# Rebuilding the last, short chunk of a speech joint kernel: one grad_out load, gradient row layouts by TensorE, x rows in another tile, and a transfer-grouping rule limited to the middle

## The chip, the cores and the metric

The kernel runs on one core of a Trainium2 chip. Its time is device microseconds (us) of one execution. Engines are named as in the profile: PE is TensorE (PEld its weight loads), DVE is VectorE, ACT is ScalarE, POOL is GpSimd, SP is SyncE, which here only issues transfers ("SPq" is its queue).

## The reference

The forward part is a small speech encoder with a joint network; the kernel computes the forward output and the gradients of all seven inputs (8 outputs in bf16).

```python
h  = gelu(conv1d(x,  w1))[:, ::2, :]     # x: (2, 16000, 256), 3 taps
f  = gelu(conv1d(h,  w2))[:, ::2, :]     # (2, 4000, 256)
j  = tanh((f @ w_f)[:, :, None, :] + (g @ w_g)[:, None, :, :])   # (2, 4000, 8, 256)
out = j @ w_o                            # out_0, (2, 4000, 8, 256)
# out_1 .. out_7: gradients for x, w1, w2, g, w_f, w_g, w_o, given grad_out
```

## The kernel before

**Chunks.** The 2 x 4000 output positions are laid end to end (8000 columns) and cut into 17 chunks: one of 256 columns, fifteen of 512, and a last one of 64 (lines 254 to 284). A 512-wide chunk is A = 4 blocks of Pw = 128 columns; the last chunk, number 16, is A = 1 block of Pw = 64, with one extra column (`c.ext`) for the end of x. Chunk 8 holds the border between the two batch entries.

**Stages of a chunk.** `stage_a` computes both convolutions with GELU and its derivative, the product with w_f (FE), and row layouts of the activations (HRo, HRe, FR). `stage_j` walks over four pairs of the 8 values of u. For each pair it computes tanh (tile JT, and JR in row layout on ACT), the output (OUT_SB), the grad_out product through w_o (matmuls of GOT with WOT, line 653), the derivative on DVE (NGZ, line 674), the sum over u (ZS, line 689, whose last addition writes NGFE, line 687), and the w_o gradient, which stays in one PSUM tile, GWO, for the whole kernel. `stage_de` goes backwards: GF from NGFE (line 753), GHe and GHo from GF (lines 770 and 801), the x gradient GX (line 867), and the weight gradients: ACCF (from NFR and FR), three ACC2 (from GFR and HRe/HRo), three ACC1 (from GHeR, GHoR and the x rows X, line 896). In the last chunk each of the seven weight gradients is finished by one DVE instruction into a stage tile (line 720) and stored.

**Row layouts.** A matmul contracts over partitions, so the weight gradients need NGFE, GF, GHe and GHo with columns on partitions. `rows` (line 457) makes these (NFR, GFR, GHeR, GHoR) with one transposing transfer each on SP's queue, for all 128 partitions whatever the chunk's width. grad_out comes in by `load_go` (one transfer per pair of u: tile GO) and is turned by `load_got` (one transposing transfer per pair: tile GOT); the class "go" has 3 buffers, "got" 4. `load_x` brings x rows into class "x" (2 buffers); class "xc" (1 buffer) holds the transposed x columns that `stage_a` reads.

**Order of the work.** All instructions are collected as `Op`s and then placed by a planner, `Flow.issue` (line 105). It keeps estimated times of every engine and of the transfer ring, and places, again and again, the ready operation that can start first; among equals the lower priority number goes first. That number is a position in the stream of columns (`F.now` or `at`): chunk k's work lies around its first column, the start at numbers below 256, the last chunk around 7936 to 8300. The order that it finds is the order on each engine's queue; real waits follow from the data. For SP it has a grouping rule (lines 150 and 151): plain copies are kind "D", transposing transfers kind "T"; while the current group has less than 6000 ns (D) or 7500 ns (T) of estimated work, an operation of the other kind counts as 2500 ns later than it could be.

In iteration k of the main loop (line 1010) the planner receives the loads of chunk k, `stage_j(k)`, `stage_a(k+1)` and `stage_de(k-1)`. So the end of the kernel is `stage_j(16)` beside `stage_de(15)`, then `gg_out` (gradients of g and w_g) and `stage_de(16)`.

Of the kernel before, what the change touches and what calls it, by code (L numbers as in the profile page):

```python
# [36 lines left out]
class Flow:  # L37
# [12 lines left out]

    def __init__(self, ctx, tc):
        self.ctx, self.tc, self.ops, self.slots, self.now, self.seq = ctx, tc, [], {}, 0.0, {}

    def cls(self, name, n, any_order=False, psum=False):
        pools = [self.ctx.enter_context(self.tc.tile_pool(
# [49 lines left out]
    def issue(self):  # L105
# [20 lines left out]
        while left:  # L126
            best = None
            for e, lst in avail.items():
                t, wake, cand = T[e], self.WAKE[e], None
                for o in lst:  # L130
                    s = o.ready + wake
                    for b in o.new:
                        st = seq[b.cls]
                        if not st[2] and st[1] != b.seq:
                            s = None
                            break
                        free = [x[1] for x in slots[b.cls] if x[1] is not None]
                        if not free or (st[2] and len(free) <= self.SPARE and queue[b.cls][head[b.cls]] is not o):
                            s = None
                            break  # L140
                        s = max(s, min(free) + wake)
                    if s is None:
                        continue
                    if o.work:
                        q = "SW" if e == "POOL" else "HW"
                        s = max(s, lanes[q][nlane[q] % self.LANES])
                    s = max(s, t)
                    k = (s, o.prio, o, e, s)

                    if e == "SP" and kind is not None and o.kind != kind and group < self.GROUP[kind]:  # L150
                        k = (s + self.WAIT,) + k[1:]
                    if cand is None or k < cand:
                        cand = k
                if cand is not None and (best is None or cand[0] < best[0]):
                    best = cand
            assert best is not None, "no operation can start"
            _, _, o, e, s = best
            for x in o.eng:
                avail[x].remove(o)
            for b in o.new:  # L160
                free = [i for i, x in enumerate(slots[b.cls]) if x[1] is not None]
                i = min(free, key=lambda i: (slots[b.cls][i][1], i))
                b.slot, slots[b.cls][i][1] = i, None
                seq[b.cls][1] += 1
                b.t = slots[b.cls][i][0].tile(b.shape, b.dtype, name=b.name, tag=b.cls)
            T[e] = s + o.cost[o.eng.index(e)]
            if o.work:

                if e == "SP":
                    group = o.work + (group if o.kind == kind else 0.0)  # L170
                    if o.kind == "T" and kind == "D":
                        ring += self.SKEW
                    kind = o.kind
                if o.kind == "T":
                    ring = max(ring, s + 300.0) + o.work
                    T[e] = max(T[e], ring - 1500.0)
                    o.done = ring + 1600.0 + self.SLACK
                else:
                    ring = max(ring, T[e] + 500.0) + o.work
                    if e == "SP":  # L180
                        T[e] = max(T[e], ring - self.HOLD)
                    o.done = ring + (2200.0 if e == "POOL" else 1300.0) + self.SLACK
                q = "SW" if e == "POOL" else "HW"
                lanes[q][nlane[q] % self.LANES] = o.done
                nlane[q] += 1
            else:
                o.done = T[e] + self.TAIL[e]
            o.span = (s, T[e], e)
            for c, q in queue.items():
                while head[c] < len(q) and q[head[c]].span is not None:  # L190
                    head[c] += 1
            o.fn(e)
            left -= 1
            for b in o.bufs:
                b.users -= 1
                if b.users == 0 and b.cls is not None:
                    slots[b.cls][b.slot][1] = o.done
            for d in o.succ:
                d.left -= 1
                if d.left == 0:  # L200
                    put(d)
# [16 lines left out]
def kernel(  # L218
# [28 lines left out]
    KT = 2  # L247
# [158 lines left out]
    def load_go(k, up, at, after=()):  # L406
        c = chunks[k]
        A, Pw = c.A, c.Pw
        GO = buf("go", [P, NB, 2, V], BF16, "GO")
        dma("SP", lambda: GO[:Pw, 0:A].rearrange("p a u v -> p a (u v)"),  # L410
            lambda: bass.AP(tensor=go_.tensor, offset=go_.offset + (c.c0 * U + 2 * up) * V,
                            ap=[[A * U * V, Pw], [U * V, A], [1, 2 * V]]),
            r=[], w=[GO], bytes_=Pw * A * 1024, new=[GO], at=at, after=after)
        st[k].setdefault("GO", {})[up] = GO

    def load_got(k, up, at):
        c = chunks[k]
        A, Pw = c.A, c.Pw
        GO = st[k]["GO"][up]
        GOT = buf("got", [P, NB, 2, KT, P], BF16, "GOT")  # L420
        dma("SP", lambda: GOT[:, 0:A, :, :, :Pw].rearrange("p a u k c -> p (a u k) c"),
            lambda: GO[:Pw, 0:A].rearrange("p a u v -> p (a u v)"), r=[GO], w=[GOT],
            bytes_=Pw * A * 1024, new=[GOT], transpose=True, at=at)
        st[k].setdefault("GOT", {})[up] = GOT

    def load_x(k, at, after=()):
# [3 lines left out]
        for h in range((A + 1) // 2):  # L430
            nb = min(2, A - 2 * h)
            nr = 4 * nb + 1
            X = buf("x", [P, 9, D], BF16, "X")
            row = 4 * c.c0 - 3 + 8 * h
            lo, new = 0, [X]
            if c.first and h == 0:
# [5 lines left out]
                    lambda row=row, nr=nr: row_ap(x_, row + 4 * A, 4 * A, 15, nr), r=[], w=[(X, "c")],  # L442
                    bytes_=15 * nr * 512, at=at, after=after)
                lo = 16
            if c.last and h == 0:
                p0 = c.Pw // 32 * 32
                zero(lambda X=X, p0=p0: X[p0:c.Pw + 1], [(X, "m")], new=new, at=at)
                new = []
                dma("SP", lambda X=X: X[c.Pw:c.Pw + 1, 0:3], lambda: x[B - 1:B, T - 3:T, :], r=[(X, "m")], w=[(X, "b")],
                    bytes_=1536, at=at, after=after)  # L450
            dma("SP", lambda X=X, lo=lo, nr=nr: X[lo:c.Pw, 0:nr].rearrange("p f d -> p (f d)"),
                lambda row=row, lo=lo, nr=nr: row_ap(x_, row + 4 * A * lo, 4 * A, c.Pw - lo, nr),
                r=[], w=[(X, "m")], bytes_=(c.Pw - lo) * nr * 512, new=new, at=at, after=after)
            tiles.append(X)
        return tiles

    def rows(k, cls, name, SRC, lo, n, r, at=None):
        R = buf(cls, [P, n if cls != "hro" else NB + 1, D], BF16, name)
        dma("SP", lambda: R[:, 0:n].rearrange("p a (k d) -> p (a k) d", d=P),
            lambda: SRC[:, lo:lo + n].rearrange("p a k c -> p (a k c)"), r=[SRC] if r is None else r, w=[R],  # L460
            bytes_=n * 65536, new=[R], transpose=True, at=at)
        return R

# [137 lines left out]
    def stage_j(k, t0, dt, GEB):  # L601
# [5 lines left out]
        def pair(up):  # L607
            F.now = tu = t0 + dt * up / UP
            q = dt / UP
            JT = buf("jt", [P, 2, KT, CW], BF16, "JT")  # L610
            GOT, GO = S["GOT"].pop(up), S["GO"].pop(up)
            for j in range(2):
                for mt in range(KT):
                    def jt(e, j=j, mt=mt):
# [8 lines left out]
            for h, tbs in enumerate(halves):  # L623
# [11 lines left out]
                def gwo(e, tbs=tbs, JR=JR):  # L635
                    for tb, m in tbs:
                        for j in range(2):
                            for d2 in range(KT):
                                n = gwo_cnt[0]
                                mm(GWO[:, d2, :], JR[:m, tb % 2, j, d2 * P:(d2 + 1) * P], GO[:m, tb, j, :],  # L640
                                   n == 0, n == n_gwo - 1)
                                gwo_cnt[0] = n + 1
                op("PE", c_pe([V] * (4 * n)), gwo, r=[JR, GO], w=[], at=tu + q * (h / 2 + 0.3))
# [1 line left out]
            for step in range(4):  # L645
# [4 lines left out]

                def gj(e, j=j, d2=d2, ps=ps):
                    for kt in range(KT):
                        mm(fl(ps[:, :W], A), WOT[:, kt, d2 * P:(d2 + 1) * P], GOT[:, 0:A, j, kt, :Pw], kt == 0, kt == KT - 1)
                NGZ = buf("ngz", [P, CW], FP32, "NGZ") if u else None
                op("PE", c_pe([W] * KT), gj, r=[GOT, WOT], w=[ps], new=[ps, NGZ] if u else [ps])
                if d2 == 0:
# [75 lines left out]
    def stage_de(k, t0, dt):  # L732
# [27 lines left out]
            lambda: pv["GF"][:, q.A, :, q.Pw - 1:q.Pw], [(pv["GF"], 0), (pv["GF"], 1)]))  # L760
        if Pw < P:
            zero(lambda: GF[:, 1:NB + 1, :, Pw:P], [(GF, "z")])
        NFR = rows(k, "rows", "NFR", NGFE, 0, A, None)
        GFR = rows(k, "rows", "GFR", GF, 1, A, [(GF, 0), (GF, 1), (GF, "z")])
        for mt in range(KT):
            ps = psum()

# [67 lines left out]
            wgrad(ACC2, i, lambda i=i: ACC2[:, i], [(rl(S[nm], da), rr(GFR), c.blk, [S[nm], GFR])], out_3[i])  # L835
            tick()
        X = load_x(k, t0 + dt * 0.2, [gf_op])
        GHeR = rows(k, "rows", "GHeR", GHe, 1, A, [(GHe, 0), (GHe, 1), (GHe, "z")])
        GHoR = rows(k, "rows", "GHoR", GHo, 0, A, None)
        tick()  # L840
        tick()
        GHz = GHzR = None
# [167 lines left out]
    for k in range(NG + 1):  # L1010
        c = chunks[min(k, NG - 1)]
        t0, Wk = (c.t0, float(c.W)) if k < NG else (float(NP), 300.0)
        if k < NG:
            for up in range(UP):
                load_go(k, up, t0 + Wk * (up / UP - 0.7), [xh] if k == 0 else [])
                load_got(k, up, t0 + Wk * (up / UP - 0.5))
        if k + 1 < NG:
# [18 lines left out]
        if k == NG - 1:  # L1036
            F.now = t0 + Wk
            gg_out()
    ctx.enter_context(tc.manual_schedule())
    F.issue()  # L1040

# [29 lines left out]
```

## Time and profile before

| What | Value |
|---|---|
| runs | 827.14 us (median of 3: 826.3 to 828.6) |
| profiled execution | 827.89 us, of which the profiled span is 826.1 us |
| busy share of the span | PE 95%, DVE 89%, ACT 86%, POOL 8% |
| 800 to 810 us | PE busy 7.51 us, DVE 5.60, ACT 3.25 |
| 810 to 820 us | PE busy 4.01 us, DVE 2.57, ACT 1.19 |
| 820 to 826 us | PE busy 2.32 us, DVE 2.06, ACT 0 |
| granted PE clock, whole span | 0.989 |

A line of the timeline gives the start in us, the length from there to the end of the group in us, the engine, the line of the kernel, the operation and its tiles (out<-in), and how many instructions were merged; square brackets tell how long the engine was idle before it and what released it. A piece of the chain of waits has start, length and what ran or was waited for. Rows of stages give for each engine the busy time (and instructions), then the granted PE clock as a share of the full one, the busy share of the transfer engines, and GB/s.

### The profile page before, as it was taken

The page shows a single profiled execution, that of the slowest core. Times are in us where ns is not written, and L with a number is a line of the kernel's source. Part 1 is how long each engine was busy: PE and PEld are TensorE (multiplying, and loading weights), DVE is VectorE, ACT ScalarE, POOL GpSimd, SP SyncE. Part 2 cuts the span into 40 slices and gives each one's busy share as a digit, 9 for nine tenths or more (in the row PEclk, how much of TensorE's full clock was granted, in tenths as well). Part 3 has the DMA queues.
Part 4 walks back from the last instruction along what each step waited for, and adds up shares of the span by engine and source line. Part 5 has one row for each costly group of instructions (what it writes and reads, how often), then busy time and mean ns, then how long its engine had stood idle before and what let it go on. Part 6 is the DMA issues. An engine that isn't in the chain of part 4 may idle for free.

```text
span 826.1 us, 15874 instructions
## 1 busy us (share of the span) xinstructions
PE 781.9 (95%) x5754; PEld 551.0 (67%) x5754; DVE 732.0 (89%) x1633; ACT 713.0 (86%) x1152; POOL 62.1 (8%) x179
## 2 busy tenths in 40 slices
PE   8889999999999999989999999999899999999984
PEld 5545667676766757757677686767668576777762
DVE  5889998998979889889899998989799898999843
ACT  5999999989888988989899899898989989898631
POOL 2000010101001010100100101010010100001011
PEclk9999999999999999999999999999999999999996
DMA  8998999999999999999998999999999999999563
GB/s 179 226 218 195 237 259 220 254 214 268 198 242 230 192 275 201 243 263 223 205 242 227 214 256 242 217 274 194 261 239 204 260 240 232 224 257 237 138 185 86
DMA packets 406099, 185.24 MB, mean 224 GB/s; under 512 B 329762, under 2 KB 397892, under 8 KB 406020
## 3 DMA queue, kind: packets, MB, share of 16 engines
q1 hardware_dynamic: 405076, 183.56, 100.3%
q8 instruction: 45, 0.74, 0.4%
q10 hardware_dynamic: 784, 0.39, 0.2%
q14 instruction: 34, 0.28, 0.1%
q0 software_dynamic: 160, 0.27, 0.1%
HBM read 52.40 MB, written 50.34 MB: 124 GB/s over the span
## 4 chain that ended last, share of the span: by engine, by line
PE 43%; DVE 24%; ACT 19%; DMA 7%; issue 4%; SPq 1%; DVEq 0%; ACTq 0%
PE ps L330 36%; PE GWO L330 6%; ACT JT L616 5%; DVE NGZ L674 4%; DMA out_dram<-OUT_SB 4%; ACT JR L632 4%; DVE g_s L480 3%; DVE ZS L689 3%; ACT JSQ L661 3%; DVE JR L627 2%; ACT OUT_SB L339 2%; DVE ACC L728 2%; ACT g_sq L475 2%; DVE g_sq L493 1%; ACT GX_SB L341 1%
## 5 line engine op out<-in xcount | busy, mean ns | idle before, releaser
L616 ACT ACTIVATE JT<-FE,GE 128x512 bf16<-128x512 bf16 (+4 forms) x288 | 180.1, 683 | 0.0
L339 ACT CAST OUT_SB<-ps 128x512 bf16<-128x512 f32 x212 | 126.7, 602 | 36.6 <-PE ps L330 27.5
L330 PE MATMUL ps<-WO,JT 128*128 128x256 bf16 (+1 forms) x1008 | 150.8, 273 | 5.9 <-DVE g_s L480 2.6
L330 PE MATMUL ps<-GOT,WOT 128*128 128x512 bf16 (+2 forms) x544 | 150.1, 362 | 6.5 <-ACT OUT_SB L339 2.7
L632 ACT ACTIVATE JR<-JR 128x1024 bf16<-128x1024 bf16 (+1 forms) x128 | 136.3, 1068 | 21.2 <-DVE JR L627 21.0
L674 DVE SCALAR_TENSOR_TENSOR NGZ<-JSQ,ps 128x512 f32<-128x512 bf16 (+3 forms) x252 | 152.1, 610 | 1.5 <-PE ps L330 1.3
L330 PEld LDWEIGHTS <-JT 128*128 128x128 bf16 (+1 forms) x1008 | 97.9, 98 | 66.1 <-issue 11.7
L330 PE MATMUL GWO<-GO,JR 128*128 128x256 bf16 (+1 forms) x1008 | 131.9, 274 | 6.2 <-ACT JR L632 5.3
L689 DVE TENSOR_TENSOR ZS<-ZS,NGZ 128x512 f32<-128x512 f32 (+2 forms) x204 | 130.8, 643 | 0.6
L661 ACT ACTIVATE JSQ<-JT 128x1024 bf16<-128x1024 bf16 (+2 forms) x116 | 118.1, 1018 | 7.3 <-DVE NGZ L674 6.5
L330 PEld LDWEIGHTS <-JR 128*128 128x128 bf16 (+1 forms) x1008 | 97.8, 98 | 27.0 <-ACT JR L632 9.3
L330 PEld LDWEIGHTS <-W 128*128 128x128 bf16 x612 | 58.5, 99 | 66.2 <-issue 9.1
L480 DVE SCALAR_TENSOR_TENSOR g_s<-g_sq,ps 128x512 bf16<-128x512 bf16 (+2 forms) x102 | 65.3, 641 | 36.1 <-ACT HTo L477 31.1
L330 PE MATMUL ps<-XC,W 128*128 128x512 bf16 (+2 forms) x408 | 88.4, 368 | 4.8 <-DVE ZS L674 2.0
L627 DVE TENSOR_TENSOR JR<-FER,GEB 128x1024 bf16<-128x1024 bf16 (+1 forms) x128 | 86.7, 679 | 1.5 <-PE GWO L330 1.5
L330 PEld LDWEIGHTS <-X 128*128 128x128 bf16 (+1 forms) x756 | 74.1, 99 | 12.2 <-DMA GHoR<-GHo 1.7
L728 DVE TENSOR_TENSOR ACC<-ACC,ps 128x512 f32<-128x512 f32 x90 | 60.5, 683 | 23.9 <-PE ps L330 23.7
L330 PE MATMUL ps<-W1T,GHe 128*128 128x256 bf16 (+1 forms) x376 | 72.5, 275 | 0.5 <-DVE ACC L728 0.5
L330 PE MATMUL ps<-W1T,GHo 128*128 128x256 bf16 (+1 forms) x378 | 72.9, 275 | 0.0
L330 PEld LDWEIGHTS <-WOT 128*128 128x128 bf16 x544 | 51.4, 98 | 32.1 <-issue 11.0
L341 ACT ACTIVATE GX_SB<-ps 128x512 bf16<-128x512 f32 (+1 forms) x105 | 63.1, 625 | 7.5 <-DMA GHoR<-GHo 4.3
L475 ACT ACTIVATE g_sq<-ps 128x512 bf16<-128x512 f32 (+2 forms) x102 | 57.8, 569 | 11.4 <-PE ps L330 10.8
(119 smaller groups left out, 1075.3 us busy)
## 6 DMA issues: line engine op xcount, KB each, us to landing
GO<-in_grad_out_dram SPq DMA_DIRECT2D x60, 512.0 KB, 5.5
out_dram<-OUT_SB SPq DMA_DIRECT2D x60, 512.0 KB, 5.9
X<-in_x_dram SPq DMA_DIRECT2D x30, 576.0 KB, 7.8
out_dram<-GX_SB SPq DMA_DIRECT2D x30, 512.0 KB, 5.4
GOT<-GO SPq DMA_TRANSPOSE x68, 6.0
GO<-in_grad_out_dram SPq DMA_DIRECT2D x4, 256.0 KB, 5.1
out_dram<-OUT_SB SPq DMA_DIRECT2D x4, 256.0 KB, 4.5
XC<-in_x_dram SPq DMA_TRANSPOSE x62, 5.0
```

The source lines that it names most:

```text
L330: nc.tensor.matmul(ps_ap, lhsT=lhsT, rhs=rhs, start=start, stop=stop)
L339: nc.scalar.copy(out=dst(), in_=src())
L341: nc.scalar.activation(out=dst(), in_=src(), func=ACT.Copy, scale=scale)
L475: op("ACT", c_act(W, True), lambda e, mt=mt, ps=ps: nc.scalar.activation(out=sq[:, 0:A, mt, :Pw], in_=fl(ps[:, :W], A), func=ACT.Square, s ...
L480: op("DVE", c_dve(W), lambda e, mt=mt, ps=ps: nc.vector.scalar_tensor_tensor(out=s[:, 0:A, mt, :Pw], in0=sq[:, 0:A, mt, :Pw], scalar=1.0, ...
L616: nc.scalar.activation(out=fl(JT[:, j, mt, :W], A)[:, :, lo:hi], in_=FE[:, 0:A, mt, lo:hi], func=ACT.Tanh, bias=GE[:, b, mt, 2 * up + j:2 ...
L627: op("DVE", c_dve(n * 2 * D, 0.5), lambda e, lo=lo, n=n, m=m, JR=JR: nc.vector.tensor_tensor(out=JR[:m, 0:n], in0=S["FER"][:m, lo:lo + n]. ...
L632: op("ACT", c_act(n * 2 * D), lambda e, n=n, m=m, JR=JR: nc.scalar.activation(out=JR[:m, 0:n], in_=JR[:m, 0:n], func=ACT.Tanh), r=[JR], w= ...
L661: nc.scalar.activation(out=JSQ[:, :, :W], in_=JT[:, j, :, :W], func=ACT.Square)
L674: nc.vector.scalar_tensor_tensor(out=fl(zap(), A)[:, :, lo:hi], in0=fl(JSQ[:, d2, :W], A)[:, :, lo:hi], scalar=1.0, in1=fl(ps[:, :W], A)[: ...
L689: nc.vector.tensor_tensor(out=a, in0=a, in1=b, op=ALU.add)
L728: op("DVE", c_dve(512), lambda e: nc.vector.tensor_tensor(out=acc_ap().rearrange("p k d -> p (k d)"), in0=acc_ap().rearrange("p k d -> p ( ...
```

## The change

Six edits, all concerning the two ends of the stream:

- The last chunk's grad_out is loaded with one transfer (all four pairs, 64 partitions of 4 KB) into one GO tile, and turned by one transposing transfer into one GOT tile. `stage_j` picks its pair by index.
- The last chunk's four row layouts of gradients are made by TensorE: two transposes against the identity into a PSUM tile, and one copy from there by ACT or DVE (`evac`).
- The last chunk's x rows go into the buffer of class "xc" instead of one of class "x".
- The zeroing of that tile's last row gets a key of its own, "z"; the two loads into it depend on it.
- The GHeR and GHoR layouts pass `pe=Pe` (65 columns), NFR and GFR `pe=Pw` (64).
- The grouping rule holds only for operations with a priority number from 256 (start of chunk 1) up to 7936 (start of chunk 16).

```diff
+        self.steady = (-1e12, 1e12)
...
-                    if e == "SP" and kind is not None and o.kind != kind and group < self.GROUP[kind]:
+                    if (e == "SP" and kind is not None and o.kind != kind and group < self.GROUP[kind]
+                            and self.steady[0] <= o.prio[0] < self.steady[1]):
                         k = (s + self.WAIT,) + k[1:]
...
         GO = buf("go", [P, NB, 2, V], BF16, "GO")
+        if c.last:
+            dma("SP", lambda: GO[:Pw].rearrange("p a u v -> p (a u v)"),
+                lambda: bass.AP(tensor=go_.tensor, offset=go_.offset + c.c0 * U * V, ap=[[U * V, Pw], [1, U * V]]),
+                r=[], w=[GO], bytes_=Pw * U * V * 2, new=[GO], at=at, after=after)
+            st[k]["GO"] = {up: GO for up in range(UP)}
+            return
...
+        if c.last:
+            dma("SP", lambda: GOT[:, :, :, :, :Pw].rearrange("p a u k c -> p (a u k) c"),
+                lambda: GO[:Pw].rearrange("p a u v -> p (a u v)"), r=[GO], w=[GOT],
+                bytes_=Pw * U * V * 2, new=[GOT], transpose=True, at=at)
+            st[k]["GOT"] = {up: GOT for up in range(UP)}
+            return
...
-            X = buf("x", [P, 9, D], BF16, "X")
+            X = buf("xc" if c.last else "x", [P, 9, D], BF16, "X")
...
-                zero(lambda X=X, p0=p0: X[p0:c.Pw + 1], [(X, "m")], new=new, at=at)
+                zero(lambda X=X, p0=p0: X[p0:c.Pw + 1], [(X, "z")], new=new, at=at)
...
-    def rows(k, cls, name, SRC, lo, n, r, at=None):
+    def rows(k, cls, name, SRC, lo, n, r, at=None, pe=0):
         R = buf(cls, [P, n if cls != "hro" else NB + 1, D], BF16, name)
+        if pe:
+            tr = psum(BF16)
+
+            def trs(e):
+                for kt in range(KT):
+                    nc.tensor.transpose(out=tr[:pe, kt * P:(kt + 1) * P], in_=SRC[:, lo, kt, :pe], identity=ident[:])
+            op("PE", c_pe([P] * KT), trs, r=r + [ident], w=[tr], new=[tr], at=at)
+            evac(lambda: R[:pe, 0], lambda: tr[:pe, 0:D], D, r=[tr], w=[R], new=[R])
+            return R
...
-                                mm(GWO[:, d2, :], JR[:m, tb % 2, j, d2 * P:(d2 + 1) * P], GO[:m, tb, j, :],
+                                mm(GWO[:, d2, :], JR[:m, tb % 2, j, d2 * P:(d2 + 1) * P], GO[:m, up if c.last else tb, j, :],
...
+        if c.last:
+            NFR = rows(k, "rows", "NFR", NGFE, 0, A, [(NGFE, 0), (NGFE, 1)], pe=Pw)
+            GFR = rows(k, "rows", "GFR", GF, 1, A, [(GF, 0), (GF, 1)], pe=Pw)
...
-        GHeR = rows(k, "rows", "GHeR", GHe, 1, A, [(GHe, 0), (GHe, 1), (GHe, "z")])
-        GHoR = rows(k, "rows", "GHoR", GHo, 0, A, None)
+        GHeR = rows(k, "rows", "GHeR", GHe, 1, A, [(GHe, 0), (GHe, 1), (GHe, "z")], pe=Pe if c.last else 0)
+        GHoR = rows(k, "rows", "GHoR", GHo, 0, A, [GHo], pe=Pe if c.last else 0)
...
-            for up in range(UP):
+            for up in range(1 if c.last else UP):
                 load_go(k, up, t0 + Wk * (up / UP - 0.7), [xh] if k == 0 else [])
...
+    F.steady = (chunks[1].t0, chunks[-1].t0)
```

## The prediction

> **What bounds the kernel now.** I read the page's 40 slices first: they tell where the engines are not full. A slice is 20.65 us.
>
> ```profile
> PE   8889999999999999989999999999899999999984
> ACT  5999999989888988989899899898989989898631
> PEclk9999999999999999999999999999999999999996
> DMA  8998999999999999999998999999999999999563
> ```
>
> From slice 4 to 38 PE is at nine tenths or more nearly everywhere: the middle is PE's, and an edit to the last 64 columns can't shorten it. The last slice (from 805.5 us) has PE at four tenths, ACT at one, transfers at three, and a lower clock: nothing is full, so something is waited for. The chain of waits names it.
>
> ```profile
> 791.00 5.73 DMA X<-in_x_dram
> 796.78 6.65 PE ps L330 x58
> ...
> 813.27 1.20 SPq L354
> 814.57 1.18 SPq L354
> 815.85 1.19 SPq L354
> 817.22 2.31 DMA GHoR<-GHo
> 819.57 2.76 PE ps L330 x12
> 822.35 0.69 DVE stage L720
> ```
>
> SP issues the four transposing row layouts of chunk 16 one behind the other (1.2 us each, L354), the last lands, PE does ACC1 and DVE the last stage tile. The timeline shows what these waits cost, and what stands before them.
>
> ```profile
> 793.04 3.53 SPq L354 DMA_TRANSPOSE GOT<-GO  x2
> 803.25 0.51 PE L330 MATMUL ps<-GOT,WOT 128*128 128x64 bf16 x12
> 805.90 0.38 PE L330 MATMUL ps<-NGFE,WFT 128*128 128x64 bf16 x4 [2.14 <-DVE NGFE L687]
> 806.76 0.28 PE L935 MATMUL psb<-ident,ngb 128*8 128x128 bf16 x2
> 808.17 0.36 DVE L803 SCALAR_TENSOR_TENSOR GHo<-G1o,ps 128x65 bf16<-128x65 bf16 x2 [0.19 <-PE ps L330]
> 815.64 0.58 PE L330 MATMUL ps<-NFR,FR 64*128 64x256 bf16 x2 [4.10 <-DMA NFR<-NGFE]
> 819.57 0.40 PE L330 MATMUL ps<-GHoR,X 65*128 65x256 bf16 x1 [1.21 <-DMA GHoR<-GHo]
> ```
>
> GHo is ready at 808.53, yet PE first reads a row layout at 815.64 and the last at 819.57. Before that, PE idles 2.14 us for NGFE. The clock by stage (the column after POOL is the granted one):
>
> ```profile
> 808.00:809.00 1.00, 0.90 (x12) 0.51 (x10) 0.36 (x2) 0.42 (x2) 0.88 (x3) 0.74 0.13 33
> 810.00:811.00 1.00, 1.00 (x7) 0.82 (x6) 0.00 (x0) 0.59 (x1) 0.00 (x0) 0.50 0.51 148
> 812.00:814.00 2.00, 0.00 (x0) 0.00 (x0) 0.00 (x0) 0.17 (x1) 0.00 (x0) 1.00 0.28 65
> 816.00:818.00 2.00, 1.32 (x8) 0.72 (x6) 1.14 (x2) 0.00 (x0) 0.00 (x0) 0.50 0.22 44
> ```
>
> If the clock knows only full and half, 0.74 means half from 808.5 on; it is full again in 812 to 814 (0.55 in 811 to 812: from 811.9) and half once more later. So a thin stretch of PE is followed by a spell of some 3.4 us at half clock, and a full stretch ends it. At half clock 256-column matmuls start 0.213 us apart (819.76, 819.98, 820.19), at full clock 0.109 (795 to 803).
>
> **The change, part by part.** All terms are made against the profiled execution (827.89 us, span 826.1); it lies 0.75 us above the median of the runs, 827.14, and I apply the difference to the median.
>
> *Row layouts by TensorE (the main term).* From GHo ready (808.53) to the end of the span (826.1) are 17.57 us. Removed: four SP issues (4 x 1.2 us) and four landings. Added: eight transposes, 0.11 us apart by the row at 806.76 (0.28 for two), about 0.9 us of PE, and four copies from PSUM of 0.28 (DVE) or 0.36 (ACT), by the rows of JR<-psb 8x256 at 807.07 and 807.94; they lie on engines that are idle there. What remains is PE's own list: GX 12 matmuls, ACCF 2, ACC2 6, ACC1 12, at half clock 32 x 0.213 = 6.8 us, and the transposes 0.9: 7.7. NFR and GFR need only NGFE and GF, so their transposes and ACCF (0.8 us) fit into PE's gaps before GHo: 6.9 remain. With one spell of 3.4 us at half clock and full clock behind it, the list takes 3.4 + (6.9 - 3.4)/2 = 5.2 us. At full clock the last ACC1 groups (4 matmuls, 0.44 us) come faster than DVE's stage instructions (0.69): +0.5. Then 0.25 until the last DVE instruction, its 0.69, and 3.06 from its end (823.04) to the end of the span (issue, landing, close). Together 9.7; saving 17.57 - 9.7 = 7.9. Bounds: with full clock throughout, DVE's seven stage instructions (4.8 us) set the end, some 9 us saved. With half clock throughout 6.7; and if besides each copy and each wait for a rows buffer (3 buffers, four tiles: GHoR needs the one that ACCF frees) lies bare on the path, four times 0.6 us, 4.3. What is late next is PE, then DVE.
>
> The trace lets the clock fall after PE's gap of only 2.14 us and a thin stretch. The Trainium skill (TensorE: Matmul & The Clock Gate, Part 1) wants a whole idle window of about 3.4 us for that; by its rule the new tail, with shorter gaps, would keep full clock, and an estimate from its 2.4 GHz would put the time near 816. The row speaks against it. The same page, Part 4, says that transposes don't count as PE activity in the way matmuls do, which speaks against this change: by it the half clock could last through the tail, an estimate of 818. No stretch as dense in transposes is in this trace.
>
> *The copies in the chain GF to GHo.* GF's matmul starts at 805.90, GHo is ready 2.63 us later, and DVE and PE alternate in it. NFR's and GFR's transposes and copies are now queued among them. Bounds 0 (all in gaps) and +1.2 (two pairs of transposes and two copies, each in front of what the chain needs); I take +0.3, since PE and DVE both have gaps of 0.2 to 0.3 there.
>
> *One grad_out load and one transpose.* Removed: three loads and three transposes on SP (0.6 and 1.2 us each by the rows of small GO and GOT). The last two GOT were issued only at 793.04, so six groups of GOT matmuls (three values of u) came together at 803.25, and DVE needed 0.64 us for each u (804.06, 804.69, 805.34) while PE idled 2.14 us. The single GO can go where the first one went (771 us; a 64 KB load lands in 3.4 us, a 256 KB one in 5.1), its GOT a little after 776, and all u but the last then lie within chunk 15's work: 2 x 0.64 = 1.3 less. Bounds 0 (the planner still puts them last) and -2.14. If the larger load comes as late as the late ones did (788.5), all four pairs are late instead of two; PE's 20 us of chunk 15 work hide up to that.
>
> *Grouping off from 7936 on.* Chunk 15's X loads (576 KB) were issued at 790.37, behind four transposes and three GO/OUT copies, though their buffers were free; PE then waited 0.70 us for X, and 0.39 us for a GO at 790.59. Both waits should go: -1.1. Bounds 0 and -1.1. The transposes GFR to GHoR now share the queue with 1.2 MB of X: a transpose right behind copies held SP 4.38 us at 512.29 and 4.92 at 610.76 instead of 1.25. GHoR landed near 789.3 and is read at 795.7, so 6 us cover that.
>
> *X rows in the xc buffer.* The zeroing on POOL (2.01 us) waited until 803.31 for PE to leave an x buffer; it moves far ahead. The loads still follow GF in the plan, land 2.8 us after issue, about 809 at worst (behind the two JR stores), and ACC1 comes last on PE, at about 811. Worth 0 here, but without the edit X would land only near 811 and be late next.
>
> *Grouping off below 256.* The start (to 60 us) is set by ACT and DVE: ACT is busy 19.63 of 20 us in 20 to 40. SP's order there already follows need (XC for chunk 1 whole, then GOT, GO, OUT). I take 0, bounds -2 and +2.
>
> **Sum:** -7.9 + 0.3 - 1.3 - 1.1 = -10.0. Span 816.1, own time 817.9, on the median 817.1.
>
> **Rivals.** *A, part of the gain only:* PE's tail list waits for copies and buffers, and the GOT groups still come last: -4.3 + 1.2 - 1.1 = -4.2, 823. For it: the rows class has 3 buffers for 4 tiles. Against: ACT is idle in the last 15 us.
>
> *B, slower:* mixing kinds on SP at the start. Price: 3.4 us for each added copy-to-transpose switch (4.4 to 4.9 instead of 1.25 us, above), between 17 and 60 us, where SP issues almost without a gap. XC of chunk 2 was issued until 42.3, lands 5 us later, and is read at 49.8: 2.5 us of cover. The tail's 10.0 and this cover are eaten by 12.5 us, 3.7 switches; with five the kernel takes 831.6. Against it: ready transposes there have the lower numbers anyway.
>
> *C, another rhythm in the middle:* the planner's order repeats per chunk, with 50.3 us a chunk from 195 to 346 and 49.2 from 448 to 645. If the shifted start moves it to the other pattern for about half of the chunks, 7 x 1.1 = 7.7 us go either way: 809.4 or 824.8.
>
> *D, nothing is won:* the end moves to another wait (the stores on SP's queue, the seven stage tiles): 827.
>
> **How the numbers follow.** Forecast (813.5 to 821) 0.62; A (821 to 824.5) 0.13; C fast 0.07; C slow 0.07; D 0.03; B 0.08. The range 812 to 824 leaves out most of C, B and D, about 0.2. A measurement of this kernel can tell about 0.3%, 2.5 us, from no change: faster 0.86 (forecast, A, C fast, some of C slow), same 0.06, slower 0.08.
>
> **What would show it.** Right: no SPq L354 after the last GOT but chunk 15's; PE's gap before ps<-NFR gone; PE's matmuls back to back from GHo until some 4 us before the end, some of them 0.21 us apart; X of chunk 15 issued near 781; PE's gap before ps<-NGFE near 0.9 us. Wrong: PE gaps at psb of the row layouts, GOT matmuls still twelve together, or a shift that is already there at 450 us, which would be B or C.

## The result and the profile after

The changed kernel took **818.17 us** (median of 6 runs, 810.32 to 820.61) where the kernel before took 827.87 (6 runs), a ratio of 0.9864 [0.9814, 0.9913]. Measured again later, with both kernels on one chip, it was 816.03 against 825.74: 0.990 [0.9863, 0.9936]. By the medians 9.7 us were won both times, by the ratios 11.3 and 8.3, give or take 4 and 3 us; 10.0 were forecast.

The profiled execution of after is the fastest of its six (810.32 us, span 808.5), so its 17.6 us below the profiled execution of before are not the change's effect. The span is better cut into three. GF(15) is the start of chunk 15's first GF matmul, GF(16) that of the last chunk's:

| Profiled execution | GF(15) at | GF(15) to GF(16) | GF(16) to end | span |
|---|---|---|---|---|
| before | 779.92 | 25.98 | 20.20 | 826.1 |
| after | 772.72 | 23.21 | 12.61 | 808.5 |
| after, profiled again | 779.57 | 23.21 | 14.42 | 817.2 |

The last two columns belong to the last chunk. The second is the history of an execution: the same program reached GF(15) at 772.72 once and at 779.57 another time.

Two rows of the page's slices of after, over 808.5 us (20.2 us each):

```profile
PE   7879999999999999999999999999999998999996
PEclk9999999999999999999999999999999999999999
```

The last slice has PE at six tenths instead of four and a full clock. The chain of waits of after shows why (start, length, what ran):

```profile
797.62 2.49 PE ps L332 x24
800.11 0.34 PE psb L480 x4
800.46 1.76 PE ps L332 x16
...
802.85 0.68 DVE stage L746
```

No transfer is left in it up to DVE's last stage tile: from GF(16) on it is PE's own list, with the transposes (L480) inside. (The chain ends with the last instruction of an engine; the stores that land behind it are not in it.) The timeline gives the marks for the sums:

```profile
773.80 0.69 SPq L358 DMA_DIRECT2D X<-in_x_dram  x1
795.93 0.38 PE L332 MATMUL ps<-NGFE,WFT 128*128 128x64 bf16 x4 [1.08 <-DVE NGFE L713]
797.77 0.39 PE L332 MATMUL ps<-NFR,FR 64*128 64x256 bf16 x2
798.41 0.39 PE L332 MATMUL ps<-GFR,HRe 64*128 64x256 bf16 x2
798.74 0.42 PE L332 MATMUL ps<-GF,W2T 128*128 128x65 bf16 x8
798.84 0.69 DVE L746 SCALAR_TENSOR_TENSOR stage<-ACC,ps 128x512 bf16<-128x512 f32 x1 [0.61 <-PE ps L332]
799.45 0.35 DVE L833 SCALAR_TENSOR_TENSOR GHo<-G1o,ps 128x65 bf16<-128x65 bf16 x2
800.86 3.27 DVE L746 SCALAR_TENSOR_TENSOR stage<-ACC,ps 128x512 bf16<-128x512 f32 x5
803.30 0.96 SPq L358 DMA_DIRECT2D out_dram<-GX_SB  x2
804.36 1.44 SPq L358 DMA_DIRECT2D out_dram<-stage  x3
```

X of chunk 15 is issued 1.1 us after GF(15) (before: 10.5), PE's gap ahead of GF(16) is 1.08 instead of 2.14, GHo is ready 3.87 us after GF(16) (before: 2.63), and DVE makes the last five stage tiles without a gap. From GF(16) to PE's last matmul the timeline lists no wait of PE.

### The profile page after: what moved, and what is told of

Same layout as the page of the kernel before. It is cut to its first block, busy times and chain, and to the rows that moved or that the text cites. A ratio compares the mean times of both kernels' runs of the same rounds, so it can differ in the third digit from the quotient of the medians.

```text
span 808.5 us, 15878 instructions
## 1 busy us (share of the span) xinstructions
PE 775.2 (96%) x5762; PEld 548.4 (68%) x5762; DVE 732.1 (91%) x1634; ACT 714.9 (88%) x1155; POOL 62.1 (8%) x179
## 4 chain that ended last, share of the span: by engine, by line
PE 41%; DVE 28%; ACT 18%; DMA 6%; issue 4%; SPq 2%; DVEq 0%; ACTq 0%
PE ps L332 35%; PE GWO L332 6%; DVE NGZ L700 5%; DMA out_dram<-OUT_SB 5%; ACT JT L642 4%; DVE ZS L715 4%; DVE g_s L505 4%; ACT JR L658 3%; ACT JSQ L687 3%; DVE ACC L754 2%; DVE JR L653 2%; ACT OUT_SB L341 2%; ACT g_sq L500 2%; DVE g_sq L518 2%; SPq L356 1%
## 5 line engine op out<-in xcount | busy, mean ns | idle before, releaser
L341 ACT CAST OUT_SB<-ps 128x512 bf16<-128x512 f32 (+1 forms) x211 | 126.2, 600 | 32.9 <-PE ps L332 25.9
L754 DVE TENSOR_TENSOR ACC<-ACC,ps 128x512 f32<-128x512 f32 x90 | 60.7, 683 | 18.9 <-PE ps L332 18.9
L500 ACT ACTIVATE g_sq<-ps 128x512 bf16<-128x512 f32 (+2 forms) x102 | 57.4, 566 | 10.7 <-PE ps L332 9.9
```

The lines of the kernel that those rows point to most:

```text
L341: nc.scalar.copy(out=dst(), in_=src())
L500: op("ACT", c_act(W, True), lambda e, mt=mt, ps=ps: nc.scalar.activation(out=sq[:, 0:A, mt, :Pw], in_=fl(ps[:, :W], A), func=ACT.Square, s ...
L754: op("DVE", c_dve(512), lambda e: nc.vector.tensor_tensor(out=acc_ap().rearrange("p k d -> p (k d)"), in0=acc_ap().rearrange("p k d -> p ( ...
```

## The experiments

Times are medians, with the ratio to the kernel before on the same chip. "Tail" is GF(16) to the end of the span, "stretch" GF(15) to GF(16).

| Run | Time (runs) | Ratio [95%] | Stretch | Tail |
|---|---|---|---|---|
| start_only | 826.06 (12) | 1.0001 [0.9971, 1.003] | 26.38 | 18.9 |
| layouts_only | 821.58 (12) | 0.9951 [0.9922, 0.998] | 26.14 | 13.96 |
| undo_layouts | 822.01 (12) | 0.9965 [0.9936, 0.9994] | 23.21 | 20.27 |
| load_only | 822.39 (10) | 0.9956 [0.9923, 0.999] | 23.21 | 20.4 |
| group_end_only | 822.73 (10) | 0.998 [0.9951, 1.0009] | 23.51 | 20.1 |
| end_only | 818.09 (6) | 0.99 [0.9845, 0.9955] | 23.21 | 12.60 |
| undo_xc | 815.41 (6) | 0.9892 [0.9856, 0.9928] | 23.21 | 12.73 |
| act_stores | 818.56 (11) | 0.9899 [0.9862, 0.9937] | 23.21 | 14.27 |
| after_again | 816.03 (6) | 0.99 [0.9863, 0.9936] | 23.21 | 14.42 |
| act_stores_2 | 815.30 (6) | 0.9894 [0.9866, 0.9922] | 23.21 | 12.22 |
| undo_xc_2 | 814.98 (6) | 0.9872 [0.9842, 0.9902] | 23.21 | 12.8 |

The last two columns, read from one profiled execution of each run, fall into few values, while single times of one kernel differ by up to 10 us and more. So the parts are told apart by these columns. The medians are much coarser (an interval is some 2.5 us or more to each side); they agree with the columns within it.

**Theory:** the tail (row layouts) and the stretch (load, grouping at the end) carry the gain; the start carries none. **Rivals:** a new rhythm of the middle, or the gain only in part.

**start_only**: before, with the grouping lifted at the start alone.

```diff
+    F.steady = (chunks[1].t0, 1e12)
```

> The kernel before with the grouping rule lifted for priorities below 256 and nothing else. Theory T (the gain lies in the last 50 us): ratio to before within 0.3% of 1, the stretch from chunk 15's GF matmul (779.92 in before) to the end stays 46 us; whatever the start shows, up or down by 1 to 3 us, differs from execution to execution. Rival S (the reordered start gives a third or more of the gain): 3 to 6 us less than before, with every execution's chunk 3 earlier by that much.

Ratio 1.0001: nothing is won or lost, to within some 2.5 us. The stretch and the tail make 45.3 us, where 46 were expected; the tail of 18.9 against 20.20 is the clock's doing, since here the half clock begins 6.6 us after GF(16), behind the GX matmuls, and in before 2.6 us after it. The order of SP's 474 transfers in before differs from that in after only among the first 113 and the last 48, and PE's matmuls 1141 to 5510 of 5754 come in the same order too. So the planner gave the middle no new rhythm, and that rival falls.

**layouts_only**: before, with the TensorE row layouts alone.

```diff
+            NFR = rows(k, "rows", "NFR", NGFE, 0, A, [(NGFE, 0), (NGFE, 1)], pe=Pw)
...
+        GHoR = rows(k, "rows", "GHoR", GHo, 0, A, [GHo], pe=Pe if c.last else 0)
```

> The kernel before with the four row layouts of the last chunk made by TensorE and nothing else. T: from chunk 16's GF matmul to the end 20.2 us become 12.5 to 13.5 (after: 12.6), the time falls by 7 to 8 us (ratio 0.991). S: the stretch shrinks by less than 4 us, since X lands late or PE waits for the copies, and the ratio stays above 0.995.

The tail falls from 20.2 to 13.96 though half of it ran at half clock (6.8 us); the stretch stays at 26.14. The expectation for the time is missed: the ratio is 0.9951, some 4 us, where 0.991 was expected, and its interval leaves 0.991 out. The 6.2 us that this profile's tail lost lie just inside it. By the letter the median is on rival S's side (above 0.995), but the tail is not (it lost 6.2 us, and S has less than 4). That the row layouts alone would win after's 7.6 us at full clock is not shown. From the timeline of this run:

```profile
794.21 0.39 PE L330 MATMUL ps<-GHoR,X 128*128 128x256 bf16 x2 [0.69 <-DMA X<-in_x_dram]
803.33 0.38 PE L330 MATMUL ps<-NGFE,WFT 128*128 128x64 bf16 x4 [2.14 <-DVE NGFE L696]
```

The waits for X and for NGFE stand as in before: the row layouts don't touch them.

**undo_layouts**: after, with the four transposing transfers again.

```diff
...
-        GHoR = rows(k, "rows", "GHoR", GHo, 0, A, [GHo], pe=Pe if c.last else 0)
+        GHoR = rows(k, "rows", "GHoR", GHo, 0, A, [GHo], pe=0)
```

> The changed kernel with the four row layouts made by transposing transfers again. T: from chunk 16's GF matmul to the end 18 to 20 us again (12.6 in after), 2 to 3 us below before in all (ratio 0.997). S: still 5 us or more below before (ratio 0.994 or less).

The counterpart: stretch 23.21, tail 20.27. The timeline:

```profile
799.83 0.36 DVE L833 SCALAR_TENSOR_TENSOR GHo<-G1o,ps 128x65 bf16<-128x65 bf16 x2 [0.19 <-PE ps L332]
801.53 0.58 PE L332 MATMUL ps<-NFR,FR 64*128 64x256 bf16 x2 [1.14 <-DMA NFR<-NGFE]
811.44 0.37 PE L332 MATMUL ps<-GHoR,X 65*128 65x256 bf16 x1 [5.23 <-DMA out_dram<-GX_SB]
```

NFR's and GFR's transposes are issued 7 us earlier after GF(16) than in before, but GHoR's comes behind stores on SP's queue, 11.4 us after GF(16) (before: 11.3), and lands at 811.30; PE idles 5.23 us for it ahead of ACC1. (The bracket names the GX store; the landing just before PE starts is GHoR's.) GHo is ready at 800.19, 2.63 us after GF(16), as in before. The ratio, 0.9965, is as expected.

**load_only** and **group_end_only**: before, with one grad_out load and transpose alone, and with the grouping lifted from 7936 on alone.

```diff
...
-            for up in range(UP):
+            for up in range(1 if c.last else UP):
```

```diff
+    F.steady = (-1e12, chunks[-1].t0)
```

> The kernel before with the last chunk's grad_out in one load and one transpose and nothing else. T, as the prediction had it: PE's gap before chunk 16's GF matmul falls from 2.14 to about 0.9 us, since only the last value of u comes behind ACC1, and the wait for a late GO goes; the stretch from chunk 15's GF matmul to chunk 16's falls from 26.0 to 24 to 24.7 us; the wait for chunk 15's X stays; the tail stays 20.2. Rival G (the 2.8 us that this stretch lost come from the lifted grouping): 26 us stay.

> The kernel before with the grouping rule lifted from 7936 on and nothing else. T: chunk 15's X is issued near chunk 15's GF matmul instead of 10 us behind it, PE's wait of 0.7 us for it goes, the stretch from GF to GF falls by 0.7 to 1.1 us (26.0 to 25), the gap of 2.14 us stays; the tail's four transposes stay on SP, 19 to 21 us. G: the whole 2.8 us go here, 23.2 us. In all 1 to 3 us below before, ratio 0.997 to 0.999.

Load alone brings the stretch to 23.21, grouping alone to 23.51; both together to 23.21. From the timeline of load_only:

```profile
780.95 0.55 SPq L356 DMA_DIRECT2D X<-in_x_dram  x1
803.55 0.38 PE L330 MATMUL ps<-NGFE,WFT 128*128 128x64 bf16 x4 [1.08 <-DVE NGFE L701]
```

Without the six SP instructions of the other three pairs, X is issued 0.6 us after GF(15), although the grouping rule still holds. And of group_end_only:

```profile
779.88 1.18 SPq L356 DMA_TRANSPOSE GOT<-GO  x1
797.33 0.38 PE L332 MATMUL ps<-NGFE,WFT 128*128 128x64 bf16 x4 [1.08 <-DVE NGFE L689]
```

With four loads and four transposes, but ungrouped, a GOT is issued at 779.88 and none later, where before the last two came at 793.04 (13.1 us after GF(15), here 6.1). Either edit removes the waits for X and for the late GO and halves the one for NGFE. Both expectations missed here: each gave its edit only a part.

**end_only** and **undo_xc**: after, without the lifted grouping at the start, and after, with X of the last chunk in class "x".

```diff
-    F.steady = (chunks[1].t0, chunks[-1].t0)
+    F.steady = (-1e12, chunks[-1].t0)
```

```diff
-            X = buf("xc" if c.last else "x", [P, 9, D], BF16, "X")
+            X = buf("x", [P, 9, D], BF16, "X")
```

> The changed kernel with the grouping rule back for the start (lifted only from 7936 on). T: as the changed kernel, ratio to before 0.987 to 0.990, since the start is worth nothing. S: 3 to 6 us of the 9.7 are lost, ratio 0.992 to 0.996.

> The changed kernel with the last chunk's x rows in a buffer of class x again. POOL's zeroing waits for ACC1 of chunk 15 and SP's queue waits for POOL, so X is issued some 6 us later than in after. T, as the prediction had it: X becomes the late one and ACC1 waits for up to 2 us, tail 12.6 to 14.6 us. Rival N (the edit is worth nothing): X lands in time, tail 12.6 us.

> The changed kernel with the x rows of the last chunk in class x again, once more, beside the changed kernel on the same chip. Theory (the edit is worth nothing): within 1.5 us of the changed kernel of this call, tail 12.6 to 12.8 at full clock. Rival (the edit costs what the earlier medians differ by, 818.2 against 815.4): 2 to 3 us below it.

end_only has after's stretch and tail and, within the intervals, after's time: the start is worth nothing that can be told. undo_xc keeps them to within 0.2 us as well. Its timeline:

```profile
804.90 0.84 SPq L358 DMA_DIRECT2D X<-in_x_dram  x2
810.00 0.27 PE L332 MATMUL ps<-GHoR,X 65*128 65x256 bf16 x1
```

X is issued 5.1 us ahead of its first use, and PE doesn't wait. On the same chip the median of undo_xc_2 lies 1.05 us below that of after_again. undo_xc ran on another chip than after did; its ratio to before, 0.9892, compares with 0.9864 and 0.990. All these intervals overlap: the buffer is worth nothing that can be told, and no version here is shown to beat after.

**act_stores**, **act_stores_2** and **after_again**: in after, SP issues GX (803.30) and three stage stores (804.36) one behind the other, and the end comes 4.41 us after DVE's last instruction (804.13) instead of 3.06. Does this queue cost 1.25 us?

```diff
-            dma("SP", lambda: out.rearrange("(dt p) n -> p dt n", p=P),
+            dma("ACT" if ACC is ACC1 else "SP", lambda: out.rearrange("(dt p) n -> p dt n", p=P),
```

> The changed kernel with the three ACC1 stores issued by ACT instead of SP. In after the last DVE instruction ends 4.4 us before the end of the span (3.06 in before), since SP still has the two GX stores and three stage stores to issue. If SP's queue sets the end, the 4.4 us fall to 3.0 to 3.4 and the tail to 11.2 to 11.6 us; if the landings of the stores set it, the tail stays 12.6. The time itself can't tell a difference of 1 us (0.12%).

> The changed kernel with ACC1's three stage stores issued by ACT, once more. Theory (the stores' queue on SP adds 1.25 us to the end, the half clock in the tail varies by itself): from the last DVE instruction to the end of the span 3.1 to 3.2 us again; tail 11.4 us if the clock stays full in it, 14.2 if not; time 1.2 us below the changed kernel of this call. Rival (issuing on ACT brings the half clock): again about 14.2 us with a clock near 0.5 to 0.7 in the microseconds after GHo.

> The changed kernel once more, with nothing edited, to see what varies from execution to execution. Theory (the gain sits in the tail and in the 26 us before it; the lead that the profiled execution of the changed kernel already had at chunk 15 was an execution's luck): median 816.5 to 819.5, GF(15) to GF(16) 23.2 us, GF(16) to the end of the span 12.6 us at full clock or 14.0 to 14.5 us with a spell at half clock, and the start of chunk 15's GF at 774 to 781 us instead of 772.7. Rival (the lifted grouping makes the middle faster): chunk 15's GF again at about 773 us.

The first run seemed to say yes (3.16 us from DVE's end to the end of the span), but its tail ran 6.8 us at half clock and was longer, 14.27. The second had full clock: 4.03 us, and a tail of 12.22, where 3.1 to 3.2 and 11.4 were expected, so ACT's queue is worth 0.39 us. In after SP's queue does hold the last store back: its tile is ready at 804.13, it is issued 1.24 us later, behind the other two of the row at 804.36, and lands in 1.9 us, with the transfer engines not full (clock, transfer share and GB/s are the last three columns):

```profile
804.90:805.90 1.00, 0.00 (x0) 0.00 (x0) 0.00 (x0) 0.00 (x0) 0.00 (x0) 1.00 0.70 184
```

In act_stores_2 ACT issues the last store 0.03 us behind its tile, but now the transfers limit:

```profile
809.70:810.70 1.00, 0.00 (x0) 0.00 (x0) 0.15 (x1) 0.00 (x0) 0.00 (x0) 1.00 1.04 266
810.70:811.70 1.00, 0.00 (x0) 0.00 (x0) 0.00 (x0) 0.00 (x0) 0.00 (x0) 1.00 0.97 216
```

The transfer engines are full after DVE's end (809.85), and the three ACT stores take 2.8 us from issue to landing. At half clock DVE's tiles come later, the stores spread out, and each lands sooner: 1.8 us in act_stores. So freeing the queue wins 1.2 us and the fuller transfers take 0.8 of them back; the first run, at half clock, could not show this.

after_again settles the clock. The program and the order of PE's instructions are after's, the gap ahead of GF(16) is again 1.08 us, and yet the chain of waits reads:

```profile
804.47 3.71 PE ps L332 x24
808.19 0.57 PE psb L480 x4
808.75 3.35 PE ps L332 x16
```

24, 4 and 16 instructions take 3.71, 0.57 and 3.35 us, in after 2.49, 0.34 and 1.76. The rows of stages say why (the clock is the third number from the end):

```profile
804.80:805.80 1.00, 1.00 (x6) 0.23 (x4) 0.28 (x2) 0.28 (x1) 0.72 (x3) 0.63 0.04 8
...
810.80:811.80 1.00, 1.00 (x7) 0.72 (x6) 0.00 (x0) 0.45 (x1) 0.00 (x0) 0.50 0.85 244
811.80:812.80 1.00, 1.00 (x10) 0.79 (x8) 0.67 (x2) 0.14 (x1) 0.00 (x0) 0.96 0.18 52
```

Worked out from 0.63 and 0.96 as shares of full and half, the half clock lasts from 805.06 to 811.88, 6.82 us. It costs the tail 14.42 - 12.61 = 1.8 us. The rival that ACT's stores brought the half clock falls: after_again has it without them, and act_stores_2 has them without it. The rival that the middle got faster falls as well: GF(15) came at 779.57. (The median, 816.03, lies just below the 816.5 to 819.5 expected.)

## Why the prediction was right

*Row layouts, -7.9 predicted, together with the copies in the chain +0.3.* The tail went from 20.20 to 12.61, -7.6, the predicted sum to the digit. That is luck: both terms were off and cancel, and in after_again the same program's tail lost only 5.78.

The copies: GF(16) to GHo ready took 3.87 instead of 2.63, **+1.24** and not +0.3. This equals my upper bound, but not by what I made the bound of. In after the last matmuls that GHo needs start at 798.74, 2.81 us after GF(16); in before it was 1.94:

```profile
807.84 0.42 PE L330 MATMUL ps<-GF,W2T 128*128 128x65 bf16 x8
```

PE ran these in the order of its queue, and of the 0.87 us GF's two transposes are 0.23, ACCF (797.77) 0.32 and the first two ACC2 matmuls (798.41) 0.32. The other 0.37 are DVE's: it made a stage tile (798.84) ahead of GHo. NFR's transposes and the four copies cost the chain nothing, and the w_g matmuls stood ahead of GHo in before too. So the step that failed is that ACCF and the transposes fit into PE's gaps before GHo, and that DVE's stage tile was at nothing in the sum. Part of the +1.24 is only moved: ACCF and some of ACC2 are then missing behind GHo.

From GHo ready to the end: 8.74 us instead of 17.57, **-8.8** instead of -7.9. My 9.7 had a spell of half clock and 3.06 us after DVE. The trace has full clock, so DVE's end comes 4.33 us after GHo, against 6.64 in my sum (5.2 + 0.5 + 0.25 + 0.69), and DVE sets the pace, as I gave for the bound. Then the last store waits in SP's queue, and the end takes 4.41 us. In after_again, with 6.82 us of half clock, the same stretch takes 10.19. So 9.7 lies between the tail at full clock and the one with 6.8 us at half. One reading of mine was wrong without harm: in the row at 806.76 two transposes of 0.22 us each take 0.28, so they start 0.06 us apart, not 0.11; with the first one's length the eight still took 0.81 us of the chain, near my 0.9.

*The clock.* "A thin stretch of PE is followed by a spell of some 3.4 us" holds as a possibility. Five profiled tails with the 1.08-us gap and the TensorE layouts stayed at full clock (after, end_only, undo_xc, undo_xc_2, act_stores_2), two had 6.8 us at half (after_again, act_stores); layouts_only, with the 2.14-us gap, fell too. The Trainium skill (TensorE: Matmul & The Clock Gate, Part 1) says that the activity window runs free, of some 3.4 us, so that one kernel differs from execution to execution: the spells of 3.4 and 6.8 us and the pair after and after_again agree. Its other rule, that the clock falls after a whole idle window, does not: PE idled 1.08 us at most in after_again. The traces bear on why. In each of them the granted clock changes only at points that lie whole multiples of 3.41 us apart (in after_again at 9.75, 47.30, 50.71, 805.06, 811.88 and 815.30). In four of the five tails at full clock such a point lies 0.4 to 1.0 us after GF(16), in the fifth (act_stores_2) 0.13 ahead of it; in the two that fell it lies 2.28 and 2.67 after it (2.69 in layouts_only), so that one stretch of 3.41 us holds most of the gap and the small matmuls of the 2.3 to 2.7 us behind it. These tails agree that this place decides; no run set it on purpose. Part 4's remark on transposes isn't borne out as a lasting half clock: eight transposes lie in the tail of after at full clock.

*Load and transpose -1.3, grouping -1.1.* The sum is right, the split is not: -2.4 predicted, -2.77 measured, but load_only has -2.77 alone and group_end_only -2.47. The step that failed is that the two terms add up. I tied X's lateness to the grouping and GOT's to the number of transfers; both come from one overfull SP queue around 787 to 796 us, and either edit relieves it. The waits themselves were priced about right: 2.14 - 1.08 = 1.06 (1.3 predicted), 0.70 and 0.39 make 2.15. The rest, 0.6, is PE's busy time: the 197 matmuls of the stretch take 22.72 us in before and 22.13 in after; why is open.

*X in the xc buffer, 0.* Right. But the remark that without the edit X would be late next was wrong: undo_xc issues X 0.73 us after GF(16) and needs it only 5.83 us after GF(16), since ACC1 is the last of PE's list.

*Start, 0.* Right, to within some 2.5 us: 1.0001.

*Rivals.* A (part of the gain) needed a tail list that waits for copies and buffers, and late GOT groups: no wait of PE is listed in after's tail, and the GOT groups came in time. D had the stores right (4.41 us instead of 3.06) but not their price. B's price was not seen in start_only. C falls by the unchanged order of the middle. But the sign that I named for B and C, a shift already there at 450 us, was a bad one: after was ahead by 9.4 us at one GF near 440 (439.94 against 449.32), after_again by 5.3, and 250 us later after_again lagged by 0.6 (694.28 against 693.70). Executions differ by that much with the same order.

*The total.* In after_again against before: 0.35 us by GF(15), 2.77 in the stretch and 5.78 in the tail, 8.9; with full clock in the tail 10.7; the medians say 9.7. How often the tail of an execution runs at half clock is not known, so the medians can't be split further.

## What to carry to other kernels

At the end of a kernel, where no engine is full, a small transposing transfer costs its issue and its landing on the path, and a handful of TensorE transposes with copies can replace it; but ask, for each instruction that the change puts ahead of the chain on its engine's queue, whether it falls into a gap (NFR's transposes here) or costs its whole price (GF's transposes, ACCF, a stage tile). Two edits that relieve the same queue don't add up: test each alone before a gain is split between them. When single executions differ by more than the gain, cut the trace at marks that all versions share and compare the pieces.

## What the runs showed of the hardware

Once the tail's PE waits were gone, seven stage tiles of 128 KB and the last GX left nearly together. From the last DVE instruction to the end it took 4.4 us with all on SP's queue, where the last store is issued 1.24 us behind its tile; 4.03 with three on ACT's, where the transfer engines are full; and 3.2 where half clock had spread the tiles (after_again on SP's queue 3.19, act_stores with ACT's 3.16).

The granted clock of one program is no fixed thing: between 45 and 50 us it was 1.00 in after and 0.73 in after_again, the same program (and 0.73 in before). Runs of one kernel on one core spread by some 10 us (810.32 to 820.61), as large as the whole effect studied; where in the middle an execution gains or loses them stays open, beyond such spells.
